# RetNet attention and a GELU feed-forward layer on one core: from step 8 on, a batch per partition half, with square transfers of eight heads

## The chip, the core and the metric

The kernel runs on one core of a Trainium2 chip. The core has five engines that run their own instruction streams: PE (TensorE, the matmul array), DVE (VectorE), ACT (ScalarE), POOL (GpSimd) and SP (SyncE, which here only issues DMA transfers). They work on SBUF, a memory of 128 partitions; matmuls write to PSUM, another memory of 128 partitions. The metric is the device time of one execution in microseconds (us), lower being better.

## What is computed

Two blocks follow each other. The first is a recurrent attention over 4 batches, 8 heads, 768 positions and a head size of 64, all in 32-bit floats:

```
state = gamma[h] * state + outer(k[t], v[t])        # one 64 x 64 state for each batch and head
y[t]  = q[t] @ state / sqrt(64)
```

The second takes y as x, a matrix of 3072 tokens (batch by position) by 512 (head by head size), through a feed-forward layer with 2048 hidden units:

```
h = x @ w_in ;  g = h * sigmoid(1.702 * h) ;  out = g @ w_out
```

The weights arrive as 64-bit floats and are narrowed to 32 bits in the kernel.

## The kernel before, in words

**Attention in steps.** The 768 positions are cut into 12 chunks of 64 rows, and two batches are worked on together. So there are 2 x 12 = 24 steps j; step j takes chunk c = j % 12 of batches b and b + 1. Within a chunk the recurrence is done as masked attention (`attend`, L258): a = k q^T under a decay mask (`masked`, L294, DVE), y = a v plus the share of the old state (`by_state`, L298, DVE, then `output`, L304, DVE), and the new state is the old one aged by gamma^64 (`aged`, L316: ACT in steps 0 to 7, POOL from step 8 on, L324) plus kd^T v (`updated`, L326, DVE). kd is k times a decay by row (`decay`, L245: POOL from step 8 on, L256). A call of `attend(j, f)` holds the scores of step j and the rest of step f = j - 1, up to 4 x 32 matmuls of 64 x 64.

**Transposes.** q and k have to be turned, so that the head size lies along the partitions. In steps 0 to 7 PE does this (L232). From step 8 on DVE does it (L235) with an instruction that transposes 32 x 32 blocks in place. The blocks themselves are put in their transposed places by the loads: `load`, L134 to L142, makes 16 transfers for q and 16 for k, each with four heads, 32 rows and 32 columns (16 KB). In the kernel before, the tile of a step has the two batches side by side along the positions: partition half r holds heads 4r to 4r + 3 of both batches. State and the decay mask follow the same layout. The untransposed k (`kn`) and v come by `plain` (L122), two transfers of 128 KB each: partition half i holds batch i, all eight heads along the free dimension.

**Feed-forward.** The 24 steps are grouped by four into six blocks m of 512 tokens (four chunks of two batches). Matrix products are done as a seven-product scheme for 2 x 2 blocks (Strassen's, in Winograd's form), in which the sums of operands are formed by DVE and POOL. `up` (L422) makes the hidden units for m > 1, `down` (L458) the output. `down` returns 28 units of PE work, each of 8 matmuls of 128 x 128 by 256. In the third product (units 8 to 11) each unit is followed by `sums_g` (L414), three DVE instructions (L416, L417, L418) and one on POOL (L419). Their results are the weights of the fourth product, units 12 to 15: unit 12 needs the sums that follow unit 8, and so on to unit 15, which needs those that follow unit 11.

**What sets the order.** PE's instructions run in the order in which the program writes them (`manual_schedule` for PE). On the other engines an instruction passed through `pin` or `keep_in_program_order` keeps its order among such instructions; everything else is placed by the framework's scheduler from its own model of durations, before the kernel runs. Up to the end of the long list of names (L616 to L632: steps 0 to 7, the weights, the hidden units of blocks 0 and 1) nearly all is pinned. After L635 only the square transfers and the DVE transposes are. The main loop (L641) runs the blocks m = 0 to 5; within a block, after every third unit one entry of `between` is taken, so that the steps of a later block lie among the matmuls of this one: turn(8), step(8) and turn(9) in m = 0, steps 9 to 12 in m = 1, and so on up to m = 4, in which step 23 is done. Block m = 5 has no steps among its units.

**Queues.** SP issues all loads in its order; a transfer that has to wait holds back those behind it. `late_loads` (L571), near the end of the list of names, issues q, k, kn and v of step 8 and q and k of step 9. Each `turn(j)` (L222) then asks for q and k of step j + 2, and each `step` for kn and v of the next step. POOL issues the output of blocks m < 5 (L472) among its arithmetic. The tiles of q and k in square form have two buffers, kn one, v two; the transposed q has two and the transposed k one.

Of the kernel before, what the change touches and what calls it, by code (L numbers as in the profile page):

```python
# [9 lines left out]
F32 = mybir.dt.float32  # L10
U32 = mybir.dt.uint32
AF = mybir.ActivationFunctionType
ALU = mybir.AluOpType
P = 128
# [14 lines left out]
def kernel(  # L29
# [29 lines left out]
    pe, act, dve, pool, sp = nc.tensor, nc.scalar, nc.vector, nc.gpsimd, nc.sync  # L59
    ctx.enter_context(tc.manual_schedule(engines={mybir.EngineType.PE}))  # L60

    B, H, S, D = q.shape
    NT, DM = out.shape
    DFF = moe_w_in.shape[1]
    HP = H // 2
    NC = S // D
    NCH = B // 2 * NC
    CB = 4
# [5 lines left out]
    C4 = 32  # L74
# [3 lines left out]
    const = ctx.enter_context(tc.tile_pool(name="const", bufs=1))  # L78
    one = ctx.enter_context(tc.tile_pool(name="one", bufs=1))
    two = ctx.enter_context(tc.tile_pool(name="two", bufs=2))  # L80
    ps_a = ctx.enter_context(tc.tile_pool(name="ps_a", bufs=1, space=bass.MemoryType.PSUM))
# [9 lines left out]
    X = const.tile([P, 7, 2, TH], F32, name="X")  # L91
# [3 lines left out]
    X1 = W2[:, 6].rearrange("p (s c) t -> p s c t", s=4)  # L95
    rowd = const.tile([P, HP, D], F32, name="rowd")
    row = G[0:1, 4, 0:2].rearrange("p a (h t) -> p (a h) t", t=D)
    ones = G[0:1, 4, 2, 0:P]
    cold = const.tile([P, 2 * H], F32, name="cold")
    whole = const.tile([P, HP], F32, name="whole")  # L100
    ident = const.tile([P, P], F32, name="ident")
    mask = const.tile([P, 2, HP, D], F32, name="mask")
    state = [const.tile([P, 2, HP, D], F32, name=f"state{i}") for i in range(2)]
# [4 lines left out]
    def pin(i):  # L108
        return tc.keep_in_program_order(i) if ordered[0] else i


    QKV = {}

    def load(j, what="qkv"):

        b, c = j // NC * 2, j % NC
        rows = slice(c * D, (c + 1) * D)
        keep = tc.keep_in_program_order if j < 2 * CB else lambda i: i  # L120

        def plain(name, src, tag, bufs, engine=sp):  # L122
            t = two.tile([P, H, D], F32, name=name + "_in", tag=tag, bufs=bufs)
            QKV[name, j] = t
            for i in range(2):
                keep(engine.dma_start(t[i * D:(i + 1) * D], src[b + i, :, rows, :].rearrange("h p d -> p h d")))

        if j < 2 * CB:
            if "q" in what:
                plain("q", q, "q_sq", 2)  # L130
            if "k" in what:
                plain("kn", k, "k_sq", 2, sp if j else act)
        elif "q" in what:
            for name, src in (("q", q), ("k", k)):  # L134
                t = two.tile([P, HP, P // C4, C4], F32, name=name + "_sq")
                for r0 in range(0, P, C4):
                    d0, h0 = r0 % D, r0 // D * HP
                    for n in range(P // C4):
                        t0 = c * D + n * C4 % D
                        tc.keep_in_program_order(sp.dma_start(  # L140
                            t[r0:r0 + C4, :, n], src[b + n * C4 // D, h0:h0 + HP, t0:t0 + C4, d0:d0 + C4]
                            .rearrange("h p d -> p h d")))  # L142
                QKV[name, j] = t
        if "v" in what:
            if j >= 2 * CB and c < NC - 1:
                plain("kn", k, "kn", 1)
            plain("v", v, "v", 2)
# [61 lines left out]
    QT, KT, KD, AT, TURNED, PA, PU, PY, SHARE = [{} for _ in range(9)]  # L209
# [3 lines left out]
    def home(j, name):  # L213

        at = ["qT", "kT", "kd", "at"].index(name)
        shape = [[HP, P], [HP, P], [H, D], [2, HP, D]][at]
        if j >= 2 * CB:
            return one.tile([P] + shape, F32, name=name, tag=name, bufs=[2, 1, 1, 2][at])
        t = G[:, at, j % 2 * 2:j % 2 * 2 + 2].rearrange("p s t -> p (s t)")
        return t.rearrange("p (a b c) -> p a b c", a=2, b=HP) if at == 3 else t.rearrange("p (a b) -> p a b", a=shape[0])  # L220

    def turn(j):  # L222

        QT[j], KT[j] = home(j, "qT"), home(j, "kT")
        if j < 2 * CB:

            x = QKV.pop(("q", j)), QKV["kn", j]
            TURNED[j] = p = [ps.tile([P, HP, P], F32, name="pt", tag="y") for i in range(2)]
            for n in (1, 0) if j else (0, 1):
                for s in range(HP):  # L230
                    for r in range(2):
                        pe.matmul(p[n][HALF[r], s, :], x[n][:, HP * r + s, :], ident, start=True, stop=True)  # L232
        else:
            for t, name in ((QT[j], "q"), (KT[j], "k")):
                tc.keep_in_program_order(dve.transpose(  # L235
                    t.rearrange("p h t -> p (h t)"), QKV.pop((name, j)).rearrange("p h s d -> p (h s d)")))
        if 2 * CB <= j < NCH - 2:
            load(j + 2, "qk")

# [5 lines left out]
    def decay(j):  # L245

        if j % NC == NC - 1:
            return
        KD[j] = home(j, "kd")
        x, d = QKV["kn", j], cold[:, H:2 * H, None]  # L250
        if j < 2 * CB:

            for h in range(H):
                pin(act.activation(KD[j][:, h], x[:, h], AF.Copy, scale=d[:, h]))
        else:
            pool.tensor_mul(KD[j], x, d.to_broadcast([P, H, D]))  # L256

    def attend(j, f=None):  # L258

        pa = ps_a.tile([P, 2, 2, HP, D], F32, name="pa", tag="pa")  # L260
        if j is not None:
            PA[j] = pa
            for s in range(HP):
                for r, i in TWO:
                    pe.matmul(pa[HALF[i], r, 0, s, :], KT[j][HALF[r], s, HALF[i]], QT[j][HALF[r], s, HALF[i]],  # L265
                              start=True, stop=True)
            KT.pop(j)
        if f is not None:
            c = f % NC
            old, vn, a, qt = state[c % 2], QKV.pop(("v", f)), AT.pop(f), QT.pop(f)  # L270
            if c < NC - 1:
                kd = KD.pop(f)
                for s in range(HP):
                    for i, r in TWO:
                        pe.matmul(pa[HALF[r], i, 1, s, :], kd[HALF[i], HP * r + s, :], vn[HALF[i], HP * r + s, :],  # L275
                                  start=True, stop=True)


            py = ps_a.tile([P, 2, 2, 2, P], F32, name="py", tag="py")
            if c:  # L280
                for s2 in range(2):
                    for i in range(2):
                        for r, o in TWO:
                            pe.matmul(py[HALF[o], r, 1, i, s2 * D:(s2 + 1) * D], old[HALF[r], i, 2 * s2 + o, :],  # L284
                                      qt[HALF[r], 2 * s2 + o, HALF[i]], start=True, stop=True)
            for s2 in range(2):
                for r in range(2):
                    for i, o in TWO:
                        s = 2 * s2 + o
                        pe.matmul(py[HALF[o], i, 0, r, s2 * D:(s2 + 1) * D], vn[HALF[i], HP * r + s, :],  # L290
                                  a[HALF[i], r, s, :], start=True, stop=True)
            PU[f], PY[f] = pa[:, :, 1], py

    def masked(j):  # L294
        AT[j] = home(j, "at")
        pin(dve.tensor_mul(AT[j], PA.pop(j)[:, :, 0], mask))  # L296

    def by_state(f):  # L298

        SHARE[f] = tmp = two.tile([P, 2, 2, P], F32, name="tmp", bufs=1)  # L300
        pin(dve.tensor_mul(tmp, PY[f][:, :, 1].rearrange("p r i t -> p i r t"),
                           rowd.rearrange("p (r s) t -> p r (s t)", r=2)[:, None].to_broadcast([P, 2, 2, P])))

    def output(f):  # L304
        c = f % NC
        th, t0 = f % CB // 2, f % 2 * D
        x = X1 if f // CB == 1 else X
        x = x[:, 2 * th:2 * th + 2].rearrange("p r s (i t) -> p (r s) i t", i=2)[:, :, :, t0:t0 + D]
        by = "p i r (s t) -> p (r s) i t"
        y = PY.pop(f)[:, :, 0].rearrange(by, t=D)  # L310
        if c:
            pin(dve.tensor_add(x, y, SHARE.pop(f).rearrange(by, t=D)))
        else:
            pin(act.activation(x, y, AF.Copy))

    def aged(f):  # L316

        c = f % NC
        old, new = state[c % 2], state[(c + 1) % 2]
        if f < 2 * CB:  # L320
            for s in range(HP):
                pin(act.activation(new[:, :, s], old[:, :, s], AF.Copy, scale=whole[:, s:s + 1]))
        else:
            pool.tensor_mul(new, old, whole[:, None, :, None].to_broadcast([P, 2, HP, D]))  # L324

    def updated(f):  # L326
        c = f % NC
# [199 lines left out]
    W = col_decay.shape[1]  # L527
# [43 lines left out]
    def late_loads():  # L571
        load(2 * CB, "qkv")
        load(2 * CB + 1, "qk")

    works |= {

# [17 lines left out]
    for name, i in [("0a", 0), ("0b", 1)] + [(str(p), 2 * p) for p in range(1, NFF)]:  # L594
        n = Narrow(i)
# [116 lines left out]
```

## Time and profile before

| What | Value |
|---|---|
| Median of 5 runs | 682.38 us (681.72 to 684.91) |
| The profiled execution | 684.91 us, of which its span is 683.2 us |
| Granted clock of PE | 1.00 throughout |
| PE busy | 671.5 us, 98% of the span |
| DVE, ACT, POOL busy | 305.9, 151.1, 124.9 us |
| Square transfers (L140) | 512 of 16 KB, median 0.43 us of SP each |
| Plain loads of kn and v by SP (L126) | 90 of 128 KB, median 0.63 us of SP each |
| DMA traffic | 46.55 MB, mean 68 GB/s |

The span runs from the first to the last instruction of the profiled execution; the time of an execution also has about 1.7 us around it. A timeline gives for a run of like instructions its start, its length, the engine, the line of the kernel, the operation with its operands, and in brackets how long the engine had been idle before it and who ended that. PE's matmuls overlap, and their ends are modelled, so a run's length is a little more than its place in the stream. "Waits" sum such idle times by the pair of who waited and who was waited for. SPq is the issuing of transfers on SP.

### The profile page before, as it was taken

Reading aid. Unit: us, or ns where it says so; the run is one execution under the profiler, and the core shown is the slowest. Engines: PE = TensorE matmul, PEld = TensorE weight load, DVE = VectorE, ACT = ScalarE, POOL = GpSimd, SP = SyncE. Lnnn points to the kernel's source line nnn. Section 1 sums busy time; section 2 is a strip of 40 time slices with the busy share of each in tenths; the row PEclk is TensorE's granted clock in tenths of the full one; section 3 lists DMA queues with packets and bytes.
Section 4 is the critical chain, followed back from the end, with each engine's and each line's share of the span. In section 5 each row is a group of like instructions: output and inputs, shape, how many; then the busy total and the mean of one; then the engine's idle time right before and its main releaser. Section 6 shows DMA issues by size and latency. Waiting matters only on the chain.

```text
span 683.2 us, 13807 instructions
## 1 busy us (share of the span) xinstructions
PE 671.5 (98%) x5830; PEld 559.6 (82%) x5830; DVE 305.9 (45%) x410; ACT 151.1 (22%) x301; POOL 124.9 (18%) x116
## 2 busy tenths in 40 slices
PE   7899999999999999999999999999999999999997
PEld 4788854747888888888888888888888888888886
DVE  3788881869710842221652222563222372222241
ACT  4765423321000001332000332000333000233000
POOL 3000000000367414000335100245100243000020
PEclk9999999999999999999999999999999999999999
DMA  8787641332222223301322310323310210000001
GB/s 203 205 221 219 179 142 59 123 84 35 48 34 64 59 45 87 68 8 19 71 55 63 75 33 12 72 39 82 73 38 8 57 34 32 16 0 1 16 0 47
DMA packets 140334, 46.55 MB, mean 68 GB/s; under 512 B 131824, under 2 KB 132848, under 8 KB 140272
## 3 DMA queue, kind: packets, MB, share of 16 engines
q1 hardware_dynamic: 136352, 39.10, 24.6%
q0 software_dynamic: 1760, 5.26, 2.1%
q10 hardware_dynamic: 2160, 1.31, 0.6%
q8 instruction: 46, 0.75, 0.5%
q14 instruction: 16, 0.13, 0.1%
HBM read 39.33 MB, written 6.29 MB: 67 GB/s over the span
## 4 chain that ended last, share of the span: by engine, by line
PE 88%; DVE 5%; SPq 3%; DMA 2%; issue 1%; ACT 0%
PE pd L495 37%; PE px L427 16%; PE py L427 12%; PE ph L376 8%; PE ph L388 5%; SPq L140 3%; PE pt L232 3%; PE pa L265 2%; PE pa L275 2%; PE py L290 2%; PE py L284 2%; PE pd L480 1%; DMA q_in<-in_q_dram 1%; DVE W L417 1%; DVE G L417 1%
## 5 line engine op out<-in xcount | busy, mean ns | idle before, releaser
L495 PE MATMUL pd<-W,G 128*128 128x256 f32 x1088 | 240.5, 381 | 0.4 <-DVE G L418 0.3
L495 PEld LDWEIGHTS pd<-W,G 128*128 128x128 f32 x1088 | 205.2, 190 | 29.4 <-DVE G L418 1.2
L427 PE MATMUL px<-X,W 128*128 128x256 f32 x512 | 119.0, 379 | 0.0
L427 PEld LDWEIGHTS px<-X,W 128*128 128x128 f32 x512 | 97.3, 190 | 13.2
L427 PE MATMUL py<-X,W 128*128 128x256 f32 x384 | 90.7, 379 | 0.0
L427 PEld LDWEIGHTS py<-X,W 128*128 128x128 f32 x384 | 73.0, 190 | 9.9
L376 PE MATMUL ph<-X,W 128*128 128x256 f32 x256 | 57.6, 382 | 0.0
L388 PE MATMUL ph<-W,W 128*128 128x512 f32 x128 | 55.6, 592 | 0.0
L376 PEld LDWEIGHTS ph<-X,W 128*128 128x128 f32 x256 | 48.1, 190 | 8.2 <-issue 1.6
L256 POOL TENSOR_TENSOR kd<-kn_in,cold 128x512 f32<-128x512 f32 x14 | 16.3, 1166 | 201.6 <-PE pa L275 110.0
L388 PEld LDWEIGHTS ph<-W,W 128*128 128x128 f32 x128 | 24.3, 190 | 28.9 <-issue 28.7
L419 POOL TENSOR_TENSOR G<-G 128x512 f32<-128x512 f32 x20 | 28.9, 1452 | 92.9 <-DVE G L418 91.1
L357 ACT ACTIVATE G<-G 128x512 f32<-128x512 f32 x48 | 30.2, 630 | 48.5 <-DVE G L437 29.9
L437 DVE TENSOR_TENSOR G<-py,p 128x512 f32<-128x512 f32 x16 | 11.1, 691 | 66.0 <-PE py L427 66.0
L296 DVE TENSOR_TENSOR at<-pa,mask 128x512 f32<-128x512 f32 x16 | 10.9, 683 | 60.5 <-PE pa L275 60.5
L495 PE MATMUL pd<-W,W 128*128 128x256 f32 x160 | 35.8, 381 | 0.4 <-DVE W L418 0.3
L495 PEld LDWEIGHTS pd<-W,W 128*128 128x128 f32 x160 | 30.2, 190 | 5.6 <-DVE W L418 1.2
L324 POOL TENSOR_TENSOR state<-state,whole 128x512 f32<-128x512 f32 x13 | 13.7, 1055 | 114.8 <-DVE state L332 114.6
L467 ACT ACTIVATE u<-pd 128x512 f32<-128x512 f32 x6 | 3.6, 597 | 135.6 <-PE pd L495 135.6
L472 POOL DMA_DIRECT2D out_dram<-o x20 | 14.9, 745 | 90.7 <-DVE o L471 90.7
L445 DVE TENSOR_TENSOR t<-py,u 128x512 f32<-128x512 f32 x16 | 11.1, 692 | 44.0 <-PE py L427 44.0
L193 DVE TENSOR_SCALAR W<-W 128x1024 f32<-128x1024 f32 (+1 forms) x17 | 11.2, 657 | 33.5 <-ACT W L189 33.3
(109 smaller groups left out, 643.9 us busy)
## 6 DMA issues: line engine op xcount, KB each, us to landing
W<-in_moe_w_in_dram SPq DMA_DIRECT2D x12, 512.0 KB, 5.8
v_in<-in_v_dram SPq DMA_DIRECT2D x48, 128.0 KB, 3.2
kn_in<-in_k_dram SPq DMA_DIRECT2D x42, 128.0 KB, 3.3
W<-in_moe_w_out_dram SPq DMA_DIRECT2D x10, 512.0 KB, 4.1
out_dram<-o POOLq DMA_DIRECT2D x20, 256.0 KB, 2.6
q_sq<-in_q_dram SPq DMA_DIRECT2D x256, 16.0 KB, 1.8
k_sq<-in_k_dram SPq DMA_DIRECT2D x256, 16.0 KB, 1.8
G<-in_moe_w_out_dram SPq DMA_DIRECT2D x6, 512.0 KB, 4.4
```

The costliest lines, as they stand in the source:

```text
L140: tc.keep_in_program_order(sp.dma_start(t[r0:r0 + C4, :, n], src[b + n * C4 // D, h0:h0 + HP, t0:t0 + C4, d0:d0 + C4] .rearrange("h p d -> ...
L232: pe.matmul(p[n][HALF[r], s, :], x[n][:, HP * r + s, :], ident, start=True, stop=True)
L256: pool.tensor_mul(KD[j], x, d.to_broadcast([P, H, D]))
L265: pe.matmul(pa[HALF[i], r, 0, s, :], KT[j][HALF[r], s, HALF[i]], QT[j][HALF[r], s, HALF[i]], start=True, stop=True)
L324: pool.tensor_mul(new, old, whole[:, None, :, None].to_broadcast([P, 2, HP, D]))
L357: pin(act.activation(g, h[:, i], AF.Gelu_apprx_sigmoid))
L376: pe.matmul(h[:, ab], w, X[:, 2 * th + c // 2, c % 2, :], start=(ab == 0 and c == 0), stop=(c == 3), skip_group_check=True)
L388: pe.matmul(h, w, X1[:, c // 2:4:2, c % 2, :], start=(c == 0), stop=(c == 3))
L419: pool.tensor_sub(a[1], a[1], a[0])
L427: pe.matmul(acc[:, u, :], W1[:, 2 * d + u, sa, c, :], X[:, sb, c, :], start=(start and u == 0 and c == 0), stop=(stop and c == 1), skip_gr ...
L472: (pool if m < NB - 1 else act).dma_start(rows[th, e], o)
L495: pe.matmul(p0[:, n, :], g1(m, p, sa)[:, n * P:(n + 1) * P], W2[:, sb, p, :], start=(new and p == 0 and n == 0), stop=(last and p == NP - ...
```

## The change

From step 8 on, in the kernel after, partition half u of the transposed q and k, and of the state, holds batch u with all eight heads, where before it held four heads of both batches.

- `load`: a square transfer has eight heads, 32 rows and 32 columns (32 KB). There are 8 for q and 8 for k in a step.
- `load`, `plain`: kn and v of these steps come in four transfers of 64 KB instead of two of 128 KB, since partition half r now holds heads 4r to 4r + 3 of both batches.
- `home`, `attend`, `masked`, `by_state`, `output`: other views of tiles of the same size; matmuls, vector instructions and their order in the program stay as they were in kind and number.
- `decay`, `aged`: the same POOL multiplications with other broadcasts. `aged` reads a new constant `whole_h` with one factor for each of the eight heads.
- `halves_anew`, called at the end of `late_loads`, all on POOL: a small transfer that fills `whole_h`; two copies that put the mask and the row decay of the upper partition half in the order of the lower half; two transfers from SBUF to SBUF, each of 64 partitions by 256 elements (64 KB), that carry the wrong halves of the state of step 7 into the other state buffer, on the other partition half; and two copies that put them from there into the state itself.

```diff
@@ load
             for i in range(2):
-                keep(engine.dma_start(t[i * D:(i + 1) * D], src[b + i, :, rows, :].rearrange("h p d -> p h d")))
+                if j < 2 * CB:
+                    keep(engine.dma_start(t[i * D:(i + 1) * D], src[b + i, :, rows, :].rearrange("h p d -> p h d")))
+                else:
+                    for r in range(2):
+                        keep(engine.dma_start(t[r * D:(r + 1) * D, i * HP:(i + 1) * HP],
+                                              src[b + i, r * HP:(r + 1) * HP, rows, :].rearrange("h p d -> p h d")))
...
-                t = two.tile([P, HP, P // C4, C4], F32, name=name + "_sq")
+                t = two.tile([P, H, D // C4, C4], F32, name=name + "_sq")
                 for r0 in range(0, P, C4):
-                    d0, h0 = r0 % D, r0 // D * HP
-                    for n in range(P // C4):
-                        t0 = c * D + n * C4 % D
+                    for n in range(D // C4):
+                        t0 = c * D + n * C4
                         tc.keep_in_program_order(sp.dma_start(
-                            t[r0:r0 + C4, :, n], src[b + n * C4 // D, h0:h0 + HP, t0:t0 + C4, d0:d0 + C4]
+                            t[r0:r0 + C4, :, n], src[b + r0 // D, :, t0:t0 + C4, r0 % D:r0 % D + C4]
                             .rearrange("h p d -> p h d")))
@@ decay
-            pool.tensor_mul(KD[j], x, d.to_broadcast([P, H, D]))
+            pool.tensor_mul(KD[j].rearrange("p (i s) d -> p i s d", i=2), x.rearrange("p (i s) d -> p i s d", i=2),
+                            cold[:, None, H:H + HP, None].to_broadcast([P, 2, HP, D]))
@@ masked
-        pin(dve.tensor_mul(AT[j], PA.pop(j)[:, :, 0], mask))
+        pin(dve.tensor_mul(AT[j], PA.pop(j)[:, :, 0],
+                           mask if j < 2 * CB else mask[:, 0:1].to_broadcast([P, 2, HP, D])))
@@ by_state, from step 8 on
+            SHARE[f] = tmp = two.tile([P, 4, 2, D], F32, name="tmp", bufs=1)
+            pin(dve.tensor_mul(tmp.rearrange("p a i t -> p i a t"), PY[f][:, :, 1],
+                               rowd[:, None].to_broadcast([P, 2, HP, D])))
@@ aged
-            pool.tensor_mul(new, old, whole[:, None, :, None].to_broadcast([P, 2, HP, D]))
+            pool.tensor_mul(new.rearrange("p r s d -> p (r s) d"), old.rearrange("p r s d -> p (r s) d"),
+                            whole_h[:, :, None].to_broadcast([P, H, D]))
@@ late_loads
         load(2 * CB + 1, "qk")
+        halves_anew()
+
+    def halves_anew():
+
+        pool.dma_start(whole_h, bass.AP(tensor=col_decay.tensor, offset=col_decay.offset + (D - 1) * W + H,
+                                        ap=[[0, P], [1, H]]))
+        pool.tensor_copy(mask[HALF[1], 0], mask[HALF[1], 1])
+        pool.tensor_copy(cold[HALF[1], H:H + HP], cold[HALF[1], H + HP:2 * H])
+        old, new = state[2 * CB % NC % 2], state[(2 * CB + 1) % NC % 2]
+        for u in range(2):
+            pool.dma_start(new[HALF[1 - u], u], old[HALF[u], 1 - u])
+        for u in range(2):
+            pool.tensor_copy(old[HALF[u], 1 - u], new[HALF[u], 1 - u])
```

## The prediction

> **What bounds the kernel now.** I read the page first, then the table of stages, PE's waits, and the timelines of the engines around the steps.
>
> ```profile
> span 683.2 us, 13807 instructions
> PE 671.5 (98%) x5830; PEld 559.6 (82%) x5830; DVE 305.9 (45%) x410; ACT 151.1 (22%) x301; POOL 124.9 (18%) x116
> PEclk9999999999999999999999999999999999999999
> ```
>
> PE is busy for 98% of the span at the full clock. The table of stages puts the missing 11.7 us: 5.1 in the first 20 us, 2.3 between 20 and 40, nothing from 40 to 180, 0.4 between 180 and 190, nothing again up to 630, and 3.7 after that, nearly all of it the last output. Steps 8 to 23, which the change touches, run from 160 to 570 us. All that PE's own waits show there and behind is this (the L418 lines):
>
> ```profile
> PE pd L495 <- DVE W L418: 0.3, 1, 0.3
> PE pd L495 <- DVE G L418: 0.3, 1, 0.3
> ```
>
> The second lies at 656.95 us, in block 5, which has no steps. The first is at 187.24 us, 0.28 us long. So the change can win 0.28 us from PE's waits, unless it makes PE's own work shorter; whatever it frees on SP beyond that is hidden already.
>
> **PE's work.** The calls of `attend` keep number, shape (64 x 64 by 64), order of array quarters and PSUM addresses; their operands are still runs of 64 elements. I cost this at 0.
>
> **SP.** These are the loads of steps 8 and 9, one tile of a step in a row:
>
> ```profile
> 140.76 8.64 SPq L140 DMA_DIRECT2D q_sq<-in_q_dram  x16
> 149.51 7.50 SPq L140 DMA_DIRECT2D k_sq<-in_k_dram  x16
> 157.05 7.54 SPq L140 DMA_DIRECT2D q_sq<-in_q_dram  x16
> 164.69 7.49 SPq L140 DMA_DIRECT2D k_sq<-in_k_dram  x16
> ```
>
> A transfer of 16 KB (128 pieces of 128 bytes) costs 7.50 / 16 = 0.47 us of the queue; one of 128 KB (512 pieces, L126) 1.28 / 2 = 0.64. No row has 256 pieces, the size of all new transfers. By these two rows it lies between 0.47 and 0.64; by pieces it is 0.47 + 0.17 x 128 / 384 = 0.53. A step took 32 x 0.47 + 4 x 0.64 = 17.6 us and takes 24 x 0.53 = 12.7 (11.3 to 15.4). SP saves 4.9 us a step (2.2 to 6.3). PE waits for none of these loads now, so all of it is hidden: 0. The four tiles above end after 32 x 0.53 = 17 us instead of 31.5, at 158 instead of 172.2. kn and v of step 8 go early, between 66 and 85 us; there four transfers of 0.53 for two of 0.64 are 0.84 us more a tile, beside a PE that has no idle time from 40 to 180 us and a queue that is idle in between: 0.
>
> One rule speaks against the split of kn and v. The Trainium skill, "DMA: Bandwidth & Descriptors", section "Rules for kernel authors", says of two transfers to disjoint partition halves that they serialize on the same 16 engines, and advises one transfer over all 128 partitions; each tile of kn and v goes the other way, from two transfers to four. By that rule the split buys nothing and costs two more issues a tile; the sum would be the same, as these are hidden.
>
> **DVE.** The form of every instruction stays one that has a row. `masked` and `by_state` multiply PSUM by a broadcast constant (L301, 684 ns; L296, 683 ns without broadcast), `output` reads and writes runs of 64 (L312, 680 ns). Each moves by under 0.05 us, I think (nearest rows: 672 to 703 ns); 0. What moves is the order. At the stall DVE did this:
>
> ```profile
> 171.06 0.70 DVE L235 STREAM_TRANSPOSE qT<-q_sq 128x512 f32<-128x512 f32 x1
> 171.69 0.64 DVE L296 TENSOR_TENSOR at<-pa,mask 128x512 f32<-128x512 f32 x1
> 174.99 0.69 DVE L471 TENSOR_TENSOR o<-pd,p 128x512 f32<-128x512 f32 x1 [2.66 <-PE pd L495]
> 175.60 0.70 DVE L235 STREAM_TRANSPOSE kT<-k_sq 128x512 f32<-128x512 f32 x1
> ...
> 185.54 1.64 DVE L418 TENSOR_TENSOR W<-g,W 128x512 f32<-128x512 f32 x1
> ```
>
> From 174.99 on DVE works without a pause until the L418 that PE waits for. In this chain stands the transpose of k of step 9, whose last transfer is issued at 171.7 and lands (median 1.8 us) at 173.5; in the 2.66 us of idle time before it nothing else was ready. When its loads end near 158, and land by 160 or so, the scheduler can put it ahead of 172. The chain is then 0.6 us shorter, more than 0.28: PE's wait goes. Next late would be nothing before 656.95. If the order stays, 0. I take -0.28.
>
> **POOL.** `halves_anew` adds three transfers and four copies. The three issues: 0.55 us for the small one (L567), 0.55 to 0.77 for the others (L567, L472). The exchange lands after 2.6 (L472) to 5.6 us (L567). The copies of 64 partitions by 256 have no row; the nearest are 0.24 us (128 x 128 memset) and 0.89 (the 64 x 512 selection, L556); I take half of the latter, 0.45, for three of them, and 0.15 for the tiny one. In all 0.55 + 2 x 0.66 + 2.6 + 3 x 0.45 + 0.15 = 6.0 us; with every upper end 0.55 + 2 x 0.77 + 5.6 + 4 x 0.89 = 11.3. It can start when the state of step 7 is there (129.2 us), and POOL's queue behind it looks like this:
>
> ```profile
> 129.46 1.27 POOL L324 TENSOR_TENSOR state<-state,whole 128x512 f32<-128x512 f32 x1 [113.37 <-DVE state L332]
> 175.98 0.77 POOL L472 DMA_DIRECT2D out_dram<-o  x1 [45.25 <-DVE o L471]
> ```
>
> Behind the copies, which wait for the exchange, stand `aged` of step 8 (129.46, wanted by DVE at 222.1) and the output at 175.98. 45 us of cover hide 6 to 11 us: 0. Were the cover gone, these 6 to 11 us would be paid in full.
>
> The copies can hold up DVE. While `aged` ran, the L194 at 129.86 took 1.41 us instead of 0.69. Three copies at 0.7 each are 2.1 us; DVE's next idle times are 4.8 us at 143.0 and 2.7 at 172.3, and the last weight (L204 at 160.2) is wanted by unit 3 of block 0 at 159.72 + 3 x 1.73 = 164.9. Hidden: 0.
>
> The Trainium skill, "SBUF — State Buffer", section "SBUF: two separate sides", warns that a transfer issued by POOL cannot write its descriptors while DVE runs an instruction on both read ports. Its section "A bandwidth-pool intuition that's wrong" gives 620 ns alone against 3100 beside such a copy. By these figures an estimate for three transfers is 7.4 us more; no run here shows it. The sum would not change.
>
> `decay` and `aged` swap forms: `decay` gets the broadcast that `aged` has now, and the other way round.
>
> ```profile
> L256 POOL TENSOR_TENSOR kd<-kn_in,cold 128x512 f32<-128x512 f32 x14 | 16.3, 1166 | 201.6 <-PE pa L275 110.0 <-DMA k_sq<-in_k_dram 53.4 <-DMA kn_in<-in_k_dram 14.0
> L324 POOL TENSOR_TENSOR state<-state,whole 128x512 f32<-128x512 f32 x13 | 13.7, 1055 | 114.8 <-DVE state L332 114.6 <-DVE state L330 0.2
> ```
>
> Their medians are 1042 and 1039 ns, so 0 (bounds: 1032 to 1487, what the rows span).
>
> **The sum.** The profiled execution took 684.91 us, 683.2 of span and 1.7 around it. 684.91 - 0.28 = 684.6. It was the slowest of the five; the median was 2.5 us lower, so the forecast for the median is 682.38 - 0.28 = **682.1 us**. Within 0.3%, 2.05 us (about what a measurement of this kernel can tell from no change), that is the same.
>
> **Rivals.**
>
> *Slower: the last sum of blocks 1 to 4 comes late.* In these blocks the steps lie beside `sums_g`, and unit 15 needs the last L418. In block 1:
>
> ```profile
> 236.59 1.64 DVE L417 TENSOR_TENSOR G<-G 128x512 f32<-128x512 f32 x1
> 238.16 0.68 DVE L296 TENSOR_TENSOR at<-pa,mask 128x512 f32<-128x512 f32 x1
> 238.76 0.92 DVE L418 TENSOR_TENSOR G<-G 128x512 f32<-128x512 f32 x1
> ```
>
> L418 ends at 239.68. PE's units 12 to 17 start at 234.85, so unit 15 starts at 234.85 + 3 x 1.73 = 240.04: a margin of 0.36 us, and 0.35 to 0.36 in blocks 2, 3 and 4. DVE is also held by `decay` there: POOL ran it from 237.65 to 239.14, and L418 took 0.92 instead of 0.69. If `decay` in its new form takes 1.04 us longer (double), or if earlier loads let the scheduler put one or two of DVE's instructions (0.69 each) ahead of L418, PE waits 0.69 - 0.36 = 0.33 to 2 x 0.69 - 0.36 = 1.02 us in each block: 1.3 to 4.1 in four, 683.4 to 686.2. It decides from 0.36 us on. For it: the margin is thin and the order is not pinned. Against it: both forms cost the same in the rows, and earlier loads give the two transposes in this stretch (229.81 and 230.44) a chance to move out of it, which widens the margin by 1.3 us.
>
> *The exchange lands behind POOL's long stretch.* If the scheduler puts it after 217.2 us, where POOL's row of sums and outputs ends, PE's state product (221.2) gets the state at 217.2 + 5.3 (both issues, landing, two copies) to 9 = 222.5 to 226: 1.3 to 5 us, 683.4 to 687.1. Against it: 45 us of idle POOL ahead.
>
> *The transfers save nothing.* With a cost by bytes, 32 KB would take SP twice as long. Against it: 128 KB take 0.64. SP's load would stay 17.6 us a step, the order of DVE too: 682.4.
>
> *Faster.* Only the idle time at the start is larger than 2 us: two pauses of PE at 21.0 and 24.7 us, 0.68 and 1.59, put down to "issue". If the change in what is loaded took them away, 682.1 - 2.3 = 679.8. Against it: SP's first pinned loads stay as they are.
>
> **How the numbers follow.** Forecast 0.58; late sums 0.25 (0.09 of it below 684.43, 0.16 above); exchange 0.05 (0.02 below, 0.03 above); no saving 0.07; faster by the start 0.05. So faster by over 0.3%: 0.05; within: 0.58 + 0.09 + 0.02 + 0.07 = 0.76; slower: 0.19. The forecast has the scatter of a median around it, which I put at 0.7 us from the spread of the five runs, and its own bounds of -0.28 and 0. The range from 681.2 to 684.7 holds the forecast, the case without saving and the lower part of the late sums, 8 in 10 or a little less.
>
> **What the profile after would show.** Right: PE near 671.5 us with 5830 matmuls; L140 with 256 transfers of 32 KB near 0.5 us; no wait at 187; the exchange between 129 and 176; L256 and L324 with medians near 1.04 us. Wrong: PE waiting for L418 in blocks 1 to 4, near 240, 345, 450 and 556 (the rival), or at 221 for the state; or PE's groups themselves of other durations, which I exclude.

## The result, and the profile after

The kernel after takes 686.52 us (median of 38 runs, 684.62 to 689.1). The kernel before, run beside it, takes 683.34 us (75 runs, 681.29 to 687.24). The ratio is 1.0046, with a 95% interval of 1.0038 to 1.0055: **slower by 3.2 us**, where 682.1 was forecast and the range ended at 684.7. The scatter tells as much as the medians. Of the 75 runs of before, 47 are below 684 us; of the 38 runs of after, none is. Below, the number of runs below 684 us stands beside every median.

Beside the experiments e1 to e12 before ran another 104 times, in three batches with medians of 684.74 us (e1 to e4), 684.49 (e5 to e8) and 683.77 (e9 to e12); 48 of these runs are below 684 us. Two single runs in a slow state, 876.5 us in e10 and 1425.6 us in e9, are left out below.

One warning ahead of the traces: the profiled execution of before took 684.91 us, from the upper end of its scatter, and that of after took 685.33, from the lower end of its own. These two traces differ by 0.4 us where the medians differ by 3.2. Laid side by side they nearly hide what is to be found.

The head of the page after:

```profile
span 683.6 us, 13634 instructions
PE 670.0 (98%) x5830; PEld 560.0 (82%) x5830; DVE 306.0 (45%) x410; ACT 151.3 (22%) x301; POOL 129.7 (19%) x123
```

Number of matmuls and busy time of PE are as before; POOL has 4.8 us more. PE's waits, after (engine, tile, line, who ended the wait: total, times, longest):

```profile
PE idle L570 <- POOL ident masks.py:199: 4.4, 1, 4.4
PE pt L238 <- DMA kn_in<-in_k_dram: 2.0, 1, 2.0
PE pa L277 <- DVE state L354: 1.3, 1, 1.3
...
PE pd L519 <- DVE G L442: 0.3, 1, 0.3
PE pd L519 <- DVE W L442: 0.3, 1, 0.3
```

The same view of before, of which the prediction showed the last two lines:

```profile
PE idle L546 <- POOL ident masks.py:199: 3.9, 1, 3.9
PE pa L265 <- issue: 1.6, 1, 1.6
PE pt L232 <- DMA q_in<-in_q_dram: 0.8, 1, 0.8
```

New is the wait of 2.0 us for kn_in. It lies at 18.1 us, in the transposes of step 2: 140 us ahead of the first step that the change means to touch. The steps from 8 on have no new wait. The two waits for L442, which answer to those for L418, are still there.

The timeline of PE shows the start. Before:

```profile
12.34 2.08 PE L546 MATMUL idle<-ident 128*128 128x512 f32 x2
15.41 1.12 PE L232 MATMUL pt<-ident,kn_in 128*64 128x128 f32 x16
...
19.56 1.09 PE L232 MATMUL pt<-ident,kn_in 128*64 128x128 f32 x16
43.49 7.17 PE L376 MATMUL ph<-X,W 128*128 128x256 f32 x32
```

After:

```profile
10.99 1.12 PE L570 MATMUL idle<-ident 128*128 128x512 f32 x2
17.40 0.69 PE L277 MATMUL pa<-G 64*64 64x64 f32 x32 [1.30 <-DVE state L354]
20.10 1.97 PE L238 MATMUL pt<-ident,kn_in 128*64 128x128 f32 x16 [2.00 <-DMA kn_in<-in_k_dram]
21.83 1.64 PE L238 MATMUL pt<-ident,q_in 128*64 128x128 f32 x16
43.98 7.17 PE L400 MATMUL ph<-X,W 128*128 128x256 f32 x32
```

Two things are to be seen. First, PE comes to its full speed at a time of its own in each execution: the same two warm-up matmuls took 2.08 us in the one and 1.12 in the other. This is called the late and the early clock below, by these durations; the granted clock of the windows is 1.00 in both at that time. After had the early clock and so was ahead, until at 18.1 us it ran dry. Then k of step 2 came, and the transposes took 1.97 us instead of 1.09: the clock had fallen again. The windows say so too (window, its length, busy time and instructions of PE, PEld, DVE, ACT and POOL, PE's granted clock, DMA share, GB/s). After:

```profile
5.00:10.00 5.00, 4.69 (x35) 3.06 (x33) 0.96 (x3) 1.15 (x2) 0.00 (x0) 1.00 1.25 228
20.00:25.00 5.00, 4.90 (x128) 4.65 (x128) 1.32 (x2) 3.15 (x7) 0.00 (x0) 0.70 1.02 174
```

Before:

```profile
5.00:10.00 5.00, 4.23 (x34) 3.30 (x32) 0.59 (x2) 1.15 (x2) 0.00 (x0) 1.00 1.09 251
20.00:25.00 5.00, 3.97 (x144) 3.31 (x140) 3.60 (x7) 3.55 (x9) 0.00 (x0) 1.00 0.66 149
```

In both the DMA engines are full between 5 and 10 us (shares of 1.25 and 1.09: the times of packets overlap), but after moves 228 GB/s where before moves 251. The granted clock is 0.70 between 20 and 25 us.

Second, the last line of each PE timeline is a useful **marker**: the first unbroken run of 32 matmuls of `ph`. From the marker to the end of the span it is 683.2 - 43.49 = 639.7 us before and 683.6 - 43.98 = 639.6 after. In these two traces nothing is lost behind the first 44 us. (Other traces lose a little more shortly behind the marker; they come below.)

The orders do not tell why. PE and ACT run the same instructions in the same order in both kernels. DVE has one pair exchanged, at 172 us. POOL has the transfer of `whole_h` between the two instructions that make the identity, so that the matrix is ready 0.5 us later (4.42 instead of 3.88), the exchange at 130 us, and behind it some of its `decay`s in earlier places. SP issues the same loads in the same order up to step 8.

### The profile page after: what moved, and what is told of

Read it like the earlier page. It is cut to its first block, busy times and chain, and to the rows that moved or that the text cites. A ratio compares the mean times of both kernels' runs of the same rounds, so it can differ in the third digit from the quotient of the medians.

```text
span 683.6 us, 13634 instructions
## 1 busy us (share of the span) xinstructions
PE 670.0 (98%) x5830; PEld 560.0 (82%) x5830; DVE 306.0 (45%) x410; ACT 151.3 (22%) x301; POOL 129.7 (19%) x123
## 4 chain that ended last, share of the span: by engine, by line
PE 94%; DVE 3%; DMA 2%; issue 0%; SPq 0%; ACT 0%; ACTq 0%
PE pd L519 39%; PE px L451 16%; PE py L451 12%; PE ph L400 8%; PE ph L412 8%; PE pt L238 2%; PE pa L277 2%; PE py L300 2%; PE pa L285 2%; PE py L294 2%; PE pd L504 1%; DMA kn_in<-in_k_dram 1%; DMA q_in<-in_q_dram 1%; DVE G L441 1%; DVE W L441 1%; DVE W L442 1%
## 5 line engine op out<-in xcount | busy, mean ns | idle before, releaser
L495 DVE TENSOR_TENSOR o<-pd,vv 128x512 f32<-128x512 f32 x12 | 7.7, 686 | 35.1 <-ACT vv L491 35.1
```

## The experiments

Each edit is against the kernel named in it. Ratios are to the runs of before in the same batch, on the same chip, with 95% intervals; they differ from the quotient of the two medians by up to about 0.002.

### First: the early transfer, or something else

`whole_h` is the only thing that the change adds in the first 44 us. Three theories stood at this point. *Delay*: the identity comes 0.5 us later. *Traffic*: a transfer of 128 pieces of 32 bytes gets in among the first loads. *Elsewhere*: the time goes in the parts from step 8 on. The first kernel is after, with `whole_h` filled behind the mask instead of at the very start:

```diff
+        pool.tensor_copy(mask[HALF[1], 0], mask[HALF[1], 1])
+        pool.tensor_copy(whole_h, mask[:, 0, 0, 0:H])
         pool.dma_start(whole_h, ...
-        pool.tensor_copy(mask[HALF[1], 0], mask[HALF[1], 1])
```

> The kernel after, in which the small transfer that fills whole_h can only be issued behind the copy of the mask, which waits for step 7, so that it leaves POOL's queue at the start. Start by delay (the transfer stands ahead of the end of the identity, on which PE's first matmuls wait): ratio to before 0.998 to 1.001, about 683 us. Start by traffic (its 128 small pieces hold up the first loads): the same, 0.998 to 1.001. Elsewhere (steps 8 to 23, the exchange of the state, the end): as the kernel after, 1.0046.

Measured: 1.0026 [1.0008, 1.0044], 685.9 us, 0 of 12 runs below 684. *Delay* and *traffic* fall as the whole cause: without the early transfer the time stays up, and PE waits 2.15 us for kn_in. The interval leaves room for a small part of theirs; e6 and e8 below show none.

The second is before, with the tile `whole_h` and its transfer alone:

```diff
     whole = const.tile([P, HP], F32, name="whole")
+    whole_h = const.tile([P, H], F32, name="whole_h")
...
         load(2 * CB + 1, "qk")
+        pool.dma_start(whole_h, ...
```

> The kernel before with the small transfer into whole_h alone, which nothing reads; it stands at the same place of POOL's queue as in the kernel after, between the two instructions of the identity. Start by delay and start by traffic: 1.004 to 1.005, about 686.5 us. Elsewhere: 1.000.

Measured: 1.0037 [1.0019, 1.0056], 686.68 us, 0 of 12. *Elsewhere* falls as well: none of the changed steps is in this kernel.

The third is after, with a copy from `ident` into `whole_h` ahead of the transfer, which puts the transfer behind the identity:

```diff
+        pool.tensor_copy(whole_h, ident[:, 0:H])
         pool.dma_start(whole_h, ...
```

> The kernel after with the small transfer directly behind the identity (a copy of 8 elements of the identity into whole_h goes ahead of it), so that it is as early but delays no identity. Start by delay: 0.998 to 1.001. Start by traffic: 1.004 to 1.005. Elsewhere: 1.0046.

Measured: 1.0036 [1.0019, 1.0054], 686.23 us, 0 of 12.

The fourth is before with the delay alone: POOL fills 400 elements a partition of a state buffer ahead of the identity, which comes 0.38 us later.

```diff
+        pin(pool.memset(state[0].rearrange("p r h t -> p (r h t)")[:, 0:400], 0.0))
         make_identity(...)
```

> The kernel before with a memset of 128 x 400 ahead of the identity on POOL, which by the 0.24 us of the 128 x 128 memset takes 0.5 to 0.75 us, in place of a transfer. Start by delay: 1.004 to 1.006. Start by traffic: 1.000. Elsewhere: 1.000.

Measured: 0.999 [0.997, 1.0011], 682.63 us, 10 of 12. No cost of the delay shows. All three theories had fallen. What the four slower kernels (after, e1, e2, e3) have and the others lack is the *tile* itself. It has 32 bytes a partition and stands between `whole` and `ident`. Every tile that is allocated behind it moves up by 32 bytes. In the built programs q_in and q_sq start at byte 208640 of a partition before (815 x 256) and at 208672 after; kn_in and k_sq at 204544 and 204576; v_in at 212736 and 212768. The tiles that take the loads began at multiples of 256 bytes and now begin 32 bytes behind one. A load of q, k or v is made of pieces of 256 bytes (64 elements of a row).

### Second: the address

Before, with 32 bytes of padding in the place of `whole_h`, and no transfer (a copy of eight elements at 130 us writes it):

```diff
     whole = const.tile([P, HP], F32, name="whole")
+    pad = const.tile([P, 8], F32, name="pad")
```

> The kernel before with an unused constant of 32 bytes a partition in the place of whole_h, and no transfer into it (a copy of 8 elements fills it at about 130 us). All tiles behind it, those of q, k and v among them, start 32 bytes later: from a multiple of 256 bytes to 32 behind one. Start by address (loads whose 256-byte pieces begin off a multiple of 256 take the DMA engines longer): 1.003 to 1.005. Start by traffic or by delay, and elsewhere (the work from step 8 on): 1.000, between 0.998 and 1.002.

Measured: 1.0038 [1.0022, 1.0055], 686.68 us, 0 of 12. Thirty-two bytes that nobody reads cost the whole loss.

After, with `whole_h` padded to 256 bytes:

```diff
-    whole_h = const.tile([P, H], F32, name="whole_h")
+    whole_h = const.tile([P, 64], F32, name="whole_h")[:, 0:H]
```

> The kernel after with whole_h as the first 8 columns of a tile of 256 bytes, so that the tiles behind it start at multiples of 256 again; the early small transfer stays where it is. Start by address: 0.998 to 1.002. Start by traffic or delay, and elsewhere: 1.0046.

Measured: 0.9991 [0.9975, 1.0008], 683.25 us, 9 of 12. The loss is gone. The same with the late fill of e1 as well:

> The kernel after with both: whole_h in a tile of 256 bytes, and the small transfer only behind the copy of the mask. Start by address: 0.998 to 1.001, and no slower than the aligned kernel with the early transfer; by how much that one is slower is the price of the transfer's place, 0 to 0.001. Elsewhere: 1.0046.

Measured: 0.9988 [0.997, 1.0007], 683.68 us, 8 of 12. With the early transfer (e6) and without it (e8) the ratio is the same within the intervals.

As e5, with 128 bytes (32 elements) of padding:

> The kernel before with an unused constant of 128 bytes instead of 32, so that the tiles behind it start 128 bytes off a multiple of 256. If pieces of 256 bytes are cut at multiples of 256: 1.002 to 1.005, since each is then cut in two. If only the offset within 64 or 128 bytes counts: 1.000. Without an effect of addresses: 1.000.

Measured: 1.0018 [0.9996, 1.0039], 684.65 us, 5 of 12: inconclusive, in between. As e5, with 64 bytes (16 elements):

> The kernel before with an unused constant of 64 bytes in the place of whole_h. If what counts is a cut at multiples of 256: like 32 bytes, 1.003 to 1.005, or at least above 1.002. If only the offset within 64 bytes counts: 1.000, between 0.998 and 1.002.

Measured: 1.0021 [1.0007, 1.0035], 685.76 us, 1 of 11.

### Third: which tiles

Before, with the padding at the head of the pool `two`, so that only the load tiles, `tmp` and `o` move by 32 bytes, and the identity, the mask and the state stay:

```diff
+    pad = two.tile([P, 8], F32, name="pad", bufs=1)
```

> The kernel before with an unused tile of 32 bytes at the head of the pool that holds the tiles of q, k, v and the output, so that these alone start 32 bytes off a multiple of 256; all else keeps its address. Start by address, with the loads as the place: 1.003 to 1.005. If another tile's address is the cause (the identity, the mask, the state, the transposed q and k): 1.000, between 0.998 and 1.002.

Measured: 1.0039 [1.0025, 1.0053], 686.88 us, 0 of 11. And the other way round, with the identity, the mask, the state and `kd` moved by 32 bytes and the load tiles back on a multiple of 256:

```diff
+    pad = const.tile([P, 8], F32, name="pad")
...
+    pad2 = one.tile([P, 56], F32, name="pad2")
```

> The counterpart: the kernel before with 32 unused bytes in the place of whole_h and 224 more behind the tile kd, so that the identity, the mask, the state and kd are shifted by 32 bytes as in the kernel after, while the tiles of q, k and v stand at multiples of 256. Loads as the place: 0.998 to 1.002. Another tile as the cause: 1.003 to 1.005.

Measured: 1.0015 [0.9996, 1.0034], 684.41 us, 3 of 11. The load tiles are enough for the whole loss. Whether the other tiles have a small part of their own stays unclear.

Last, after with `whole_h` padded to 128 bytes and filled late, and 128 bytes ahead of the first weight tile, so that the weights, 128 bytes off in both kernels, start at multiples of 256 too:

```diff
+    lead = const.tile([P, 32], F32, name="lead")
...
-    whole_h = const.tile([P, H], F32, name="whole_h")
+    whole_h = const.tile([P, 32], F32, name="whole_h")[:, 0:H]
```

> The kernel after with aligned loads and the late small transfer, and in addition 128 unused bytes ahead of the first weights tile, so that the raw weights (pieces of 2 and 4 KB, now 128 bytes off a multiple of 256) start at multiples of 256 too. If each piece off a multiple costs one more cut: one in eight of a 2 KB piece, at the start a part of a microsecond to 1 us off, 0.997 to 0.999 of before. If long pieces do not care: as the aligned kernels, 0.998 to 1.000.

Measured: 0.9987 [0.9972, 1.0002], 682.72 us, 10 of 12. It has the best median of the kernels with the change, but the interval holds 1.

### What the traces of the experiments show

In all, kernels whose load tiles begin 32 bytes off have 0 of 97 runs below 684 us. Of those with the load tiles on a multiple of 256, the three with the new layout (e6, e8, e11) have 27 of 36, e4 has 10 of 12, e10 3 of 11, and before 47 of 75 beside after and 48 of 104 beside the experiments.

The DMA queue that carries the loads, in the first 40 us (packets, MB, share of 16 engines), first before, with the landing of the loads of k and v by SP (issues, size, median us from issue to landing):

```profile
q1 hardware_dynamic: 17895, 7.92, 75.2%
...
kn_in<-in_k_dram SPq DMA_DIRECT2D x10, 128.0 KB, 4.9
v_in<-in_v_dram SPq DMA_DIRECT2D x10, 128.0 KB, 4.3
```

After:

```profile
q1 hardware_dynamic: 17675, 7.50, 95.3%
...
kn_in<-in_k_dram SPq DMA_DIRECT2D x10, 128.0 KB, 6.0
v_in<-in_v_dram SPq DMA_DIRECT2D x10, 128.0 KB, 7.0
```

e6 (after, aligned), e12 (before, load tiles off) and e5 (before, 32 bytes of padding), in three fences:

```profile
q1 hardware_dynamic: 18113, 8.33, 81.5%
```

```profile
q1 hardware_dynamic: 17747, 7.61, 92.3%
```

```profile
q1 hardware_dynamic: 17585, 7.31, 92.7%
```

About as many packets take the engines 95.3% of 40 us where 75.2% did. The time of one packet is share x 16 engines x 40 us / packets: 0.752 x 640 / 17895 = 26.9 ns before, 0.953 x 640 / 17675 = 34.5 ns after. The table has this for every profiled execution. "Wait" is PE's wait for k of step 2, "clock" the granted clock between 20 and 25 us, "marker" the start of the run of 32.

| Kernel | Load tiles off by | ns a packet | Wait, us | Clock | Marker, us | Marker to end, us |
|---|---|---|---|---|---|---|
| before | 0 | 26.9 | none | 1.00 | 43.49 | 639.7 |
| e4 | 0 | 28.6 | none | 1.00 | 40.34 | 639.9 |
| e6 | 0 | 28.8 | none | 1.00 | 41.20 | 639.5 |
| e8 | 0 | 27.1 | none | 1.00 | 43.12 | 639.5 |
| e10 | 0 | 27.6 | none | 1.00 | 43.69 | 639.8 |
| e11 | 0 | 27.4 | none | 0.87 | 42.41 | 639.5 |
| after | 32 | 34.5 | 2.0 | 0.70 | 43.98 | 639.6 |
| e1 | 32 | 34.2 | 2.1 | 0.66 | 43.79 | 639.7 |
| e2 | 32 | 34.1 | 0.7 | 1.00 | 43.55 | 640.8 |
| e3 | 32 | 34.0 | 2.5 | 0.50 | 45.44 | 640.2 |
| e5 | 32 | 33.7 | 1.7 | 0.66 | 43.94 | 640.9 |
| e12 | 32 | 33.3 | none | 1.00 | 44.53 | 640.3 |
| e9 | 64 | 32.7 | 1.4 | 0.66 | 43.29 | 639.7 |
| e7 | 128 | 31.4 | none | 1.00 | 42.45 | 639.8 |

Every aligned kernel lies at 26.9 to 28.8 ns, every kernel 32 bytes off at 33.3 to 34.5, with nothing between but 64 and 128 bytes off. These packets are of several sizes. Counted by size in the traces, those of 256 bytes alone take 18.5 to 19.0 ns on average in the aligned kernels in these 40 us, 26.0 to 27.4 with the tiles 32 bytes off, 25.9 at 64 and 22.9 at 128. The e7 execution waits 1.45 us for k too, but for that of step 0, at 7.7 us; there the granted clock is 0.59 and 0.73 in the two windows from 10 to 20 us.

e6 is the fair partner of after: same code, and the clock early in both profiled executions. Its PE timeline:

```profile
10.74 1.13 PE L570 MATMUL idle<-ident 128*128 128x512 f32 x2
17.16 0.69 PE L277 MATMUL pa<-G 64*64 64x64 f32 x32 [1.29 <-DVE state L354]
17.79 1.09 PE L238 MATMUL pt<-ident,kn_in 128*64 128x128 f32 x16
41.20 7.17 PE L400 MATMUL ph<-X,W 128*128 128x256 f32 x32
```

The wait of 1.29 us for DVE is there in both. But at 17.79 the transposes of k go on at once and at full clock, where after waited to 20.10 and then ran them at 1.97. The marker comes 43.98 - 41.20 = 2.78 us earlier, nearly the whole difference of the medians (3.2). Before has the late clock in its profiled execution, so that its own marker of 43.49 looks like that of after. Among the aligned kernels the executions with the late clock (before, e8) have it at 43.1 to 43.5 and those with the early one at 40.3 to 42.4 (e4, e6, e11). The exception is e10, at 43.7: its clock was early, but 16 matmuls of `ph` at 25.35 us, behind a pause of 1.5 us that is put down to "issue", took 5.22 us instead of 3.72. With the tiles 32 bytes off no execution has the marker below 43.5: what an early clock wins, the wait loses again.

e12, whose execution also has a late clock, shows the other case:

```profile
12.47 2.08 PE L547 MATMUL idle<-ident 128*128 128x512 f32 x2
15.54 1.97 PE L233 MATMUL pt<-ident,kn_in 128*64 128x128 f32 x16
44.53 7.17 PE L377 MATMUL ph<-X,W 128*128 128x256 f32 x32
```

PE does not wait for k there, and still the marker is 1.0 us behind that of before: its next transposes, at 15.54 us, took 1.97 us where before had 1.12. It came to full speed later still; why is not shown.

Four of the traces lose time a second time, behind the marker. At 53.63 us before goes on without a pause; e5 waits for v in the same place:

```profile
53.63 0.65 PE L275 MATMUL pa<-v_in,G 64*64 64x64 f32 x32
```

```profile
54.35 0.33 PE L276 MATMUL pa<-v_in,G 64*64 64x64 f32 x4
55.14 0.62 PE L276 MATMUL pa<-v_in,G 64*64 64x64 f32 x26 [0.46 <-DMA v_in<-in_v_dram]
```

In e2, e3 and e12 this wait is 0.29, 0.33 and 0.21 us long. These four are the kernels with 640.2 to 640.9 us from marker to end in the table; no aligned kernel has the wait. The trace of after does not have it either. Its span of 683.6 us is 1.0 below the median span of after's runs (684.6), so the runs in the middle may lose here too; that is not shown.

## Why the prediction was wrong, point by point

**The step that failed** is the price of `whole_h`. The prediction had it as "0.55 us for the small one" on POOL, hidden in 45 us of idle time, and said of the start: "SP's first pinned loads stay as they are." Their order and sizes did; their destinations did not. The 32 bytes a partition that the constant takes up were no term of the sum. The start was looked at for a gain only, in the rival *Faster*, although the first view of the profile had put 7.4 of the 11.7 us without PE there, and the page's DMA line had its highest digits there. A loss in that place was the missing rival. Its price, from the runs: loads of k that land after 6.0 us instead of 4.9, up to 2.5 us of wait for them, and a clock that falls for some 5 us behind it; in four traces 0.5 to 1.2 us more behind the marker; 3.2 us in the medians.

**PE's work** stayed what it was: 5830 matmuls, 639.6 us from the marker to the end against 639.7. None of the rivals beside the steps came true. In block 1 the timeline of DVE has the order of before:

```profile
237.21 1.64 DVE L441 TENSOR_TENSOR G<-G 128x512 f32<-128x512 f32 x1
238.77 0.68 DVE L306 TENSOR_TENSOR at<-pa,mask 128x512 f32<-128x512 f32 x1
239.37 0.92 DVE L442 TENSOR_TENSOR G<-G 128x512 f32<-128x512 f32 x1
```

The stretch lies 0.6 us later, as PE itself does there (235.47 instead of 234.85), and PE waits for no L442 in blocks 1 to 4.

**SP.** The loads of steps 8 and 9, after:

```profile
142.40 4.61 SPq L145 DMA_DIRECT2D q_sq<-in_q_dram  x8
147.10 4.30 SPq L145 DMA_DIRECT2D k_sq<-in_k_dram  x8
151.45 3.90 SPq L145 DMA_DIRECT2D q_sq<-in_q_dram  x8
155.45 3.85 SPq L145 DMA_DIRECT2D k_sq<-in_k_dram  x8
...
226.13 2.58 SPq L131 DMA_DIRECT2D v_in<-in_v_dram  x4
```

In the least disturbed rows a square of 256 pieces costs 3.85 / 8 = 0.48 us, a transfer of 64 KB 2.58 / 4 = 0.645; 0.53 was predicted for both. (Over all rows from step 8 on the squares take 0.54 us each on average, from 0.47 to 0.71; those of before took 0.52, from 0.46 to 0.61.) The price does not go by pieces: 128 and 256 pieces into 32 partitions cost nearly the same, and so do 256 and 512 pieces into 64. By these rows the two errors cancel: a step takes 16 x 0.48 + 8 x 0.645 = 12.8 us (predicted 12.7). The four tiles take 159.30 - 142.40 = 16.9 (predicted 17), but there two of the four rows are slower, 0.58 and 0.54 us a transfer. Both agreements are luck in part. So the saving of nearly 5 us a step is real, and it is hidden, as said: a queue was shortened that PE did not wait for. The split of kn and v cost SP what the prediction took from the rule against it (the Trainium skill, "DMA: Bandwidth & Descriptors", "Rules for kernel authors"): 64 KB cost as much as 128 KB did, so that a tile takes two issues more. Whether the transfers themselves serialize, no run here shows.

**The -0.28 us.** The transpose of kT did move ahead, as predicted, and PE's wait stayed at 0.28 us:

```profile
172.88 0.69 DVE L241 STREAM_TRANSPOSE kT<-k_sq 128x512 f32<-128x512 f32 x1
175.25 0.69 DVE L495 TENSOR_TENSOR o<-pd,p 128x512 f32<-128x512 f32 x1 [1.68 <-PE pd L519]
176.91 0.69 DVE L440 TENSOR_TENSOR X<-W,X 128x512 f32<-128x512 f32 x1 [0.96 <-PE pd L519]
...
186.16 1.64 DVE L442 TENSOR_TENSOR W<-g,W 128x512 f32<-128x512 f32 x1
```

```profile
187.86 1.99 PE L519 MATMUL pd<-W,W 128*128 128x256 f32 x8 [0.28 <-DVE W L442]
```

With the transpose out of the way, the chain of sums (L440 to L442) starts with a wait of 0.96 us for PE's own unit. Counted from the first matmul of block 0's output (160.34 us, before 159.72), it starts after 16.57 us, before after 16.56. The chain was not bound by its length alone but by PE at its head as well; the term was 0, not -0.28.

**POOL.** The exchange ran from 130.45 to 136.47:

```profile
130.45 1.36 POOL L608 DMA_DIRECT2D state<-state  x2 [50.66 <-DVE state L356]
135.04 1.43 POOL L610 COPY state<-state 64x256 f32<-64x256 f32 x2 [3.23 <-DMA state<-state]
136.56 1.89 POOL L347 TENSOR_TENSOR state<-state,whole_h 128x512 f32<-128x512 f32 x1
176.24 0.78 POOL L496 DMA_DIRECT2D out_dram<-o  x1 [37.80 <-DVE o L495]
```

That is 6.0 us, and 37.80 us of POOL's cover were left. The likeness to the predicted 6.0 us is luck: that sum also held the small transfer and two copies, which ran earlier (0.59, 0.40 and 0.18 us), so that 4.8 us of it were for this part. The landing was later (3.23 us of wait behind the issues, 2.6 predicted) and the copies of the state cost 0.70 us, not 0.45. The three issues took 0.59, 0.52 and 0.85 us of POOL, so that the 7.4 us estimated from the Trainium skill's "SBUF — State Buffer" did not show. The medians of `decay` and `aged` are 1040 and 1042 ns.

**The base.** The forecast started from 682.38, the median of five runs. Seventy-five give 683.34. A scatter of 6 us needs more than five; 1.0 us of the distance between forecast and result comes from this.

**Where the expected gain is.** With aligned loads (e6, e8, e11) the change is worth 0.9991, 0.9988 and 0.9987, all with 1 in the interval; from marker to end they take 639.5 us against 639.7. The new layout alone is the "same" that was forecast.

**The rules that bear on the cause.** The Trainium skill, "DMA: Bandwidth & Descriptors", section "How a descriptor splits into AXI transactions", has it that a transaction starts at an address aligned to 256 bytes, so that a descriptor that starts elsewhere is cut, with bytes fetched for nothing. It speaks of what is read; here the side that is written was moved. The direction agrees with the runs, the size does not: an estimate by its beats of 32 bytes has a piece of 256 bytes go from 8 to 9 at an offset of 32, to 10 at 64 and to 12 at 128, while the runs show the most at 32 (33.3 to 34.5 ns a packet), 32.7 at 64 and the least at 128 (31.4, one execution). That each offset makes two transactions of one would fit 32 and 64, not 128. Why an offset costs time, and why 32 costs more than 128, no run here shows.

## What to carry to other kernels

- A new constant is also an address. When a kernel gets slower in a place that the change does not touch, and the order of instructions is the same, compare the start addresses of the tiles; pad a small tile so that those behind it stay where they were, above all the destinations of loads in small pieces.
- Ask of every full resource of the profile, not only of the changed steps, whether the change can touch it. Time per packet (share x engines / packets) shows such a thing at a glance where landing times and waits scatter.
- Where the runs of a kernel scatter by more than the effect, two traces can come from opposite ends of their scatters. Find a marker, compare executions alike up to it, and count runs.

## What the runs showed of the hardware that was not expected

- Destinations 32 bytes behind a multiple of 256 cost 4.5 to 7.6 ns more for each packet in a full queue of mostly 256-byte pieces (33.3 to 34.5 instead of 26.9 to 28.8). Later, where the queue is a fifth busy, the shift does next to nothing: between 200 and 570 us the share is 20.3% before, 20.6% in e12, 19.6% after. Most pieces are of 128 bytes there, but those of 256 bytes alone say the same: 17.9 ns on average before, 18.2 in e12.
- SP's issue of a transfer follows, in these four shapes, the number of partitions rather than that of the pieces: in the least disturbed rows 0.47 and 0.48 us for 128 and 256 pieces into 32 partitions, 0.645 and 0.64 us for 256 and 512 pieces into 64.
- Behind a wait of 2.0 us at 18 us PE's granted clock was 0.70 between 20 and 25 us (0.50 to 0.66 in e1, e3, e5 and e9, after waits of 1.4 to 2.5 us; 1.00 in e2 after 0.7, and in e6 without the wait). Before had a pause of 1.59 us at 24.7 and kept its clock, so that the length alone does not decide.
